# A later assumed landing for the block-diagonal loads in a hand-made instruction order

## The chip, the cores and the metric

The kernel runs on one core of one Trainium2 chip. The metric is the device time of one execution in microseconds (us); less is better.

## What is computed

Three stages follow one another. A delta-rule recurrence over 768 tokens (4 batches, 8 heads, head size 48), then two feed-forward layers over the 3072 token rows (384 to 2048 to 384), the first with a softplus, the second with h·cos(h) between its two products.

```python
def _attn_ref(q, k, v, beta):
    k_n = k / (np.linalg.norm(k, axis=-1, keepdims=True) + 1e-06)
    state = np.zeros((B, H, D, D))
    for t in range(S):
        y[:, :, t] = np.einsum('bhd,bhde->bhe', q[:, :, t], state)
        v_old = np.einsum('bhde,bhd->bhe', state, kt)
        state = state + bt[:, :, :, None] * np.einsum('bhd,bhe->bhde', kt, vt - v_old)

def _moe_ref(x, w_in, w_out):       # first layer
    h = x @ w_in
    return (np.maximum(h, 0.0) + np.log1p(np.exp(-np.abs(h)))) @ w_out

def _moe2_ref(x, w_in, w_out):      # second layer
    h = x @ w_in
    return (h * np.cos(h)) @ w_out
```

## The kernel before, in words

**The work.** The recurrence is cut into 24 chunks of 32 tokens. Six groups of four chunks are prepared: `norms` (L473) loads the keys into `kt` and squares them on ScalarE, `prep` (L946) normalizes, splits into fp16 pairs and transposes, loads `bdA`, forms the chunk's Gram products in `gram` (L572) and stores what the recurrence will need to DRAM (`kqd`, `kpd`), and `solve` (L620) inverts a triangular system on VectorE and stores it to `tgd`. `step(n)` (L696) then runs one chunk: a product with the state by `bdK`, two products with `bdT` with one by `bdG` between them, the state's update and an output by `bd2`, another by `bdQ`, and a DMA transpose of the output into `xt`. Two chunks make one block of 256 tokens for the first feed-forward layer (`moe_in`, `moe_out`; 12 blocks), and pairs of those blocks make the 6 blocks of the second.

**The block-diagonal operands.** Each chunk's per-head operands stand in SBUF as block-diagonal tiles, one 32-row block for each batch, so that one 128x128 matmul serves four batches. The zeros are written once. `bd_load` (L563) fills the four blocks with four DMAs from the SP queue; `load_G` (L665) does the same for `bdG` with lines of its own. There is one buffer of each tile, so a load waits until the last matmul on the old contents is done.

**The order.** Nothing is run where it is written. `put` collects every operation with its engine, an assumed duration and the keys that it writes and reads. `Plan.run` (L246) then makes one fixed order for each engine. `tails` (L119) gives each operation a priority: the assumed time from its start to the end of the program. `greedy` (L130) walks forward through assumed time and gives each engine, whenever it is free, the ready operation of highest priority. The walk is done six times, each with priorities from a walk backward over the last order, and the order with the shortest assumed span is emitted. The chip then runs each engine's list in order, with semaphores for the dependences.

For a DMA the plan assumes an issue of 0.475 to 0.65 us on SP, and data that stands 0.65 us, the transfer and 0.9 us after it, plus `slack`. In the forward walk `end = dma_free + 0.9 + o["slack"]` (L223) is when the readers may start; in `tails` and in the walk backward `0.65 + 0.9 + o["dma"] + o["slack"]` (L117) is added to the load's own priority, and so to that of all that comes before it. The transfers assumed are 0.45 us for `bdK` and `bdQ`, 0.35 for `bdA`, 0.22 for `bdT`, 0.67 for `bd2` and 0.11 for `bdG`. `slack` is 0 except for the transposes into `xt` (8 us from chunk 3 on).

Of the kernel before, what the change touches and what calls it, by code (L numbers as in the profile page):

```python
# [20 lines left out]
P = 128  # L21
B, H, S, D = 4, 8, 768, 48
C = 32
# [259 lines left out]
def delta_moe_moe_kernel(ctx, tc, q, k, v, beta, mask, w1, w2, out):  # L283
# [39 lines left out]
    bdG = att.tile([P, H, B, X2], F16, name="bdG")  # L323
# [6 lines left out]
    y16 = att.tile([P, 2, H, D], F16, name="y16")  # L330
# [36 lines left out]
    kpd = dr.tile([NS, P, C * 56], F16, name="kpd")  # L367
# [4 lines left out]
    def put(var, w, r, fn, **kw):  # L372
        return pl.add(var, w, r, fn, **kw)

    def dma(dst, src, w, r, eng_us, issue=0.475, **kw):
        put([("SP", issue)], w, r, lambda e: nc.sync.dma_start(out=dst, in_=src), dma=eng_us, **kw)  # L376

    def copy(out, in_, scale, w, r, n, ps=False, fast=True, only=None, **kw):
        var = [("ACT", act(n, ps)), ("DVE", dve(n, fast and not ps))]
        if only:  # L380
            var = [x for x in var if x[0] in only]

        def fn(e):
            if e == "ACT":
                nc.scalar.activation(out=out, in_=in_, func=AF.Copy, scale=scale)  # L385
            elif scale == 1.0:
                nc.vector.tensor_copy(out=out, in_=in_)
            else:
                nc.vector.tensor_scalar_mul(out, in_, scale)

        put(var, w, r, fn, port=fast, **kw)
# [7 lines left out]
    def stt(out, a, s, b, op0, op1, w, r, n, **kw):  # L399
        put([("DVE", dve(n) + (0.0 if isinstance(s, (int, float)) else 0.06))], w, r,  # L400
            lambda e: nc.vector.scalar_tensor_tensor(out, in0=a, scalar=s, in1=b, op0=op0, op1=op1), port=True, **kw)  # L401
# [13 lines left out]
    A = dict(boost=BOOST)  # L415
# [130 lines left out]
    def kqd_key(n, i):  # L546
        return [("kqd", n)] if n >= 4 else [("kqd", n, i)]
# [15 lines left out]
    def bd_load(dst, key, src, r, us, issue=0.475):  # L563
        src = src.rearrange("p (x t) -> p x t", t=X2)
        for b in range(B):
            rows = slice(32 * b, 32 * b + 32)
            dma(dst[rows, :, b], src[rows], [(key, b)], r + [(key, "z")], us, issue=issue, **A)

    def bk(key):
        return [(key, b) for b in range(B)]  # L570
# [91 lines left out]
    def load_T(n):  # L662
        bd_load(bdT, "bdT", tgd[n // 4, :, n % 4], [("tgd", n // 4)], 0.22)

    def load_G(n):  # L665
        src = kpd[n, :, 48 * C:].rearrange("p (h x) -> p h x", h=H)
        for b in range(B):
            rows = slice(32 * b, 32 * b + N2)
            dma(bdG[rows, :, b, C:], src[rows], [("bdG", b)], [("kpd", n), ("bdG", "z")], 0.11, **A)


    def load_v(n):
        dma(vtb[n % 2], v[n].rearrange("p (h d) -> p h d", h=H), [("vt", n % 2)], [], 0.55, **A)

    def group(ps, key, passes, first=True, last=True):
        for i, (lhs, mov, r) in enumerate(passes):
            def fn(e, i=i, lhs=lhs, mov=mov):
                for h in range(H):
                    nc.tensor.matmul(  # L679
                        ps[:, h, 0:D], lhsT=lhs(h), rhs=mov[:, h],  # L680
                        start=(first and i == 0 and h == 0),
                        stop=(last and i == len(passes) - 1 and h == H - 1))
            put([("PE", 8 * mm(D))], [key], r, fn, cold=1.55, **A)
# [4 lines left out]
    def by_state(bd, key):  # L688

        r = bk(key)  # L690
        return ([(lambda h, l=l: col(bd, H + h, l), st16[:, m, 0], r + [("st16", m, 0)])
                 for l, m in HI_FIRST]
                + [(lambda h, l=l: col(bd, h, l), st16[:, 1, 1], r + [("st16", 1, 1)])
                   for l in range(2)])

    def step(n):  # L696
        vk = [("vt", n % 2)]
        vt = vtb[n % 2]
        if n == 0:
            copy(bt, vt, -1.0, [("bt",)], vk, DM, **A)  # L700
        else:
            r = ps_c[0]
            group(r, ("psC", 0), by_state(bdK, "bdK"))
            stt(bt, r[:, :, 0:D], 1.0 / (K_SC * S_SC), vt, ALU.mult, ALU.subtract, [("bt",)],
                [("psC", 0)] + vk, DM, **A)
        if n + 1 < NS:
            bd_load(bdK, "bdK", kqd[n + 1, :, 0:32 * C], kqd_key(n + 1, 0), 0.45)

        def take_b():
            copy(b16[:, 0], bt, S_SC, [("b16", 0)], [("bt",)], DM, **A)  # L710
            stt(b16[:, 1], bt, S_SC, b16[:, 0], ALU.mult, ALU.subtract, [("b16", 1)], [("bt",), ("b16", 0)], DM, **A)

        take_b()
        if n:
            group(ps_y, ("psY",), by_state(bdQ, "bdQ"), last=False)
        if n + 1 < NS:
            bd_load(bdQ, "bdQ", kqd[n + 1, :, 32 * C:], kqd_key(n + 1, 1), 0.45)
        if n + 2 < NS:
            load_v(n + 2)
        if n and n % 4 == 0:  # L720
            load_T(n)
        u = ps_c[1]
        uk = [("psC", 1)]
        tk = bk("bdT")

        def take_u():
            copy(u16[:, 0], u[:, :, 0:D], 1.0 / T_SC, [("u16", 0)], uk, DM, ps=True, **A)
            stt(u16[:, 1], u[:, :, 0:D], 1.0 / T_SC, u16[:, 0], ALU.mult, ALU.subtract, [("u16", 1)],
                uk + [("u16", 0)], DM, **A)

        by_T = [(lambda h, l=l: col(bdT, h, l), b16[:, m], tk + [("b16", m)]) for l, m in HI_FIRST]
        group(u, ("psC", 1), by_T)
        take_u()
        x = ps_c[0]
        group(x, ("psC", 0), [(lambda h, l=l: col(bdG, h, l), u16[:, m], bk("bdG") + [("u16", m)])
                              for l, m in HI_FIRST])
        if n + 1 < NS:
            load_G(n + 1)
        stt(bt, x[:, :, 0:D], 1.0 / (K_SC * S_SC), bt, ALU.mult, ALU.add, [("bt",)], [("psC", 0)], DM, **A)
        take_b()  # L740
        group(u, ("psC", 1), by_T)
        if (n + 1) % 4:
            load_T(n + 1)
        take_u()
        if n + 1 < NS:
            for c in range(2):
                d = ps_c[c]
                group(d, ("psC", c), [
                    (lambda h, c=c, l=l: col(bd2, (1 - c) * H + h, l), u16[:, m],
                     bk("bd2") + [("u16", m)]) for l, m in HI_FIRST])  # L750
            for c in range(2):
                stt(st[:, c], ps_c[c][:, :, 0:D], 1.0 / K_SC, st[:, c], ALU.mult, ALU.add, [("st", c)],
                    [("psC", c)], DM, **A)
                copy(st16[:, 0, c], st[:, c], 1.0, [("st16", 0, c)], [("st", c)], DM, **A)
                if c == 0:
                    tt(st16[:, 1, c], st[:, c], st16[:, 0, c], ALU.subtract, [("st16", 1, c)],
                       [("st", c), ("st16", 0, c)], DM, **A)
                else:
                    stt(st16[:, 1, c], st16[:, 0, c], mask_sb[:, C:C + 1], st[:, c], ALU.mult, ALU.add,
                        [("st16", 1, c)], [("st", c), ("st16", 0, c), ("mask",)], DM, **A)  # L760
        group(ps_y, ("psY",), [(lambda h, l=l: col(bd2, 2 * H + h, l), u16[:, m],
                                bk("bd2") + [("u16", m)]) for l, m in HI_FIRST], first=(n == 0))
        if n + 1 < NS:
            load_2(n + 1)
        sc = Y_SC / (Q_SC * S_SC)
        copy(y16[:, 0], ps_y[:, :, 0:D], sc, [("y16", 0)], [("psY",)], DM, ps=True, **A)
        stt(y16[:, 1], ps_y[:, :, 0:D], sc, y16[:, 0], ALU.mult, ALU.subtract, [("y16", 1)],
            [("psY",), ("y16", 0)], DM, **A)
        j, off = blk_of[n]
        x = xtb[j % XTB]  # L770
        put([("SP", 0.65)], [("xt", j % XTB, i) for i in range(off // P, off // P + 1)],
            [("y16", 0), ("y16", 1)],
            lambda e: nc.sync.dma_start_transpose(
                out=x[:, :, off:off + P], in_=y16.rearrange("p a h d -> p (a h d)")), dma=0.67, hold=0.55, slack=8.0 if n > 2 else 0.0, **A)


    blocks = [[n, n + 1] for n in range(0, NS, 2)]
# [147 lines left out]
    for n in range(4):  # L925
        prep_k(n)
        if n % 2:
            dst, keys = (bdKQ[:, :, 0:12], bdA22)[n // 2], [first[n - 1][1], first[n][1]]
            src = kg0[n // 2][:, :, 16 * C:].rearrange("p n (x t) -> p n x t", t=X2)
            for m in range(2):  # L930
                for b in range(B):
                    rows = slice(32 * b, 32 * b + 32)
# [6 lines left out]
    for n in range(4):  # L939
        prep_q(n)  # L940
        ps, pk = gram(n, first[n][0], first[n][1], (1,))
        take_P(n, ps[:, :, 0], pk)
    load_2(0)
    load_G(0)

    def prep(n):  # L946
# [14 lines left out]
    for g in range(NG):  # L961
# [8 lines left out]
        for n in range(4 * g, 4 * g + 4):  # L970
            step(n)
            j, off = blk_of[n]
# [55 lines left out]
```

## Time and profile before

| | us |
|---|---|
| median of 3 runs | 1060.73 |
| lowest, highest | 1059.9, 1066.73 |
| the profiled execution's own time | 1063.94 |
| its span, first to last instruction | 1062.1 |

The page of the profile gives the busy time of each engine, the share of 40 slices, the chain that ended last and the costliest groups; the trace behind it answers which wait ended last before an instruction. PE is TensorE's matmuls, PEld its weight loads, DVE is VectorE, ACT ScalarE, POOL GpSimd, SPq the queue that issues the DMAs. `bdA` and `bd2` are parts of one tile, and so are `bdK` and `bdQ`; the trace tells them by the source: `bdA<-kq` is the load of `bdA`, `bdA<-kpd` that of `bd2`, `bdKQ<-kqd` those of `bdK` and `bdQ`. PE's granted clock is given as a share of 2.4 GHz.

### The profile page before, as it was taken

The page shows a single profiled execution, that of the slowest core. Times are in us where ns is not written, and L with a number is a line of the kernel's source. Part 1 is how long each engine was busy: PE and PEld are TensorE (multiplying, and loading weights), DVE is VectorE, ACT ScalarE, POOL GpSimd, SP SyncE. Part 2 cuts the span into 40 slices and gives each one's busy share as a digit, 9 for nine tenths or more (in the row PEclk, how much of TensorE's full clock was granted, in tenths as well). Part 3 has the DMA queues.
Part 4 walks back from the last instruction along what each step waited for, and adds up shares of the span by engine and source line. Part 5 has one row for each costly group of instructions (what it writes and reads, how often), then busy time and mean ns, then how long its engine had stood idle before and what let it go on. Part 6 is the DMA issues. An engine that isn't in the chain of part 4 may idle for free.

```text
span 1062.1 us, 27812 instructions
## 1 busy us (share of the span) xinstructions
PE 946.3 (89%) x11552; PEld 687.3 (65%) x11552; DVE 656.2 (62%) x1146; ACT 681.4 (64%) x1281; POOL 404.0 (38%) x365
## 2 busy tenths in 40 slices
PE   1246769898889899999999999999999999999998
PEld 1146648797778789889988998844444444444443
DVE  7876877566836683674485675497555555555554
ACT  5455748686757676777666877976555545555554
POOL 7363526433423352252223433555223323223332
PEclk9556978999989999999999999999999999999999
DMA  8888794758754876567477972111101000010000
GB/s 246 217 219 173 162 246 113 178 129 181 174 127 69 178 170 121 84 156 168 68 148 178 215 169 83 60 45 60 60 1 60 1 30 30 1 60 1 30 1 31
DMA packets 307742, 117.94 MB, mean 111 GB/s; under 512 B 272160, under 2 KB 287648, under 8 KB 307616
## 3 DMA queue, kind: packets, MB, share of 16 engines
q1 hardware_dynamic: 307616, 116.17, 46.2%
q8 instruction: 91, 1.49, 0.6%
q14 instruction: 35, 0.29, 0.1%
HBM read 71.03 MB, written 35.65 MB: 100 GB/s over the span
## 4 chain that ended last, share of the span: by engine, by line
PE 63%; DVE 9%; DMA 8%; SPq 7%; ACT 6%; issue 4%; POOL 2%; DVEq 0%; POOLq 0%; ACTq 0%
PE psH L798 18%; PE accA L860 12%; PE accB L860 9%; PE psC L798 7%; SPq L376 7%; PE psA L860 6%; PE psC L679 5%; PE psY L798 3%; PE psY L679 2%; DMA kt<-k_dram 2%; DMA bdA<-kq 1%; DMA kpd<-kp 1%; PE psA L589 1%; DVE tmpd L397 1%; DVE tlan L397 1%
## 5 line engine op out<-in xcount | busy, mean ns | idle before, releaser
L397 POOL TENSOR_TENSOR g<-g,g 128x512 f16<-128x512 f32 x192 | 227.4, 1185 | 499.1 <-ACT g L385 489.1
L798 PE MATMUL psH<-xt,w 128*128 128x256 f16 x1728 | 238.2, 278 | 7.6 <-DVE g L397 5.9
L385 ACT ACTIVATE g<-g 128x512 f16<-128x512 f32 x192 | 120.5, 629 | 104.4 <-DVE g L401 65.4
L798 PEld LDWEIGHTS <-w 128*128 128x128 f16 x1728 | 159.5, 99 | 28.3 <-issue 8.1
L860 PEld LDWEIGHTS <-w 128*128 128x128 f16 x1728 | 162.8, 98 | 21.2 <-issue 1.6
L860 PE MATMUL accA<-g,w 128*128 128x256 f16 x1152 | 159.0, 275 | 1.1 <-POOL g L397 1.0
L860 PEld LDWEIGHTS <-v 128*128 128x128 f16 x864 | 84.5, 98 | 102.1 <-issue 0.3
L798 PEld LDWEIGHTS <-v 128*128 128x128 f16 x864 | 84.5, 98 | 101.4 <-issue 0.8
L406 ACT ACTIVATE e<-e 128x512 f32<-128x512 f32 x96 | 60.3, 629 | 84.0 <-DVE e L401 84.0
L397 DVE TENSOR_TENSOR g<-psH,e 128x512 f32<-128x512 f32 x96 | 66.1, 688 | 67.1 <-ACT e L408 59.6
L860 PE MATMUL accB<-g,w 128*128 128x256 f16 x576 | 95.0, 275 | 0.0
L798 PE MATMUL psH<-xu,v 128*128 128x512 f16 x351 | 83.3, 379 | 0.6 <-DVE g L401 0.6
L798 PE MATMUL psC<-xu,v 128*128 128x512 f16 x342 | 81.5, 379 | 0.0
L679 PE MATMUL psC<-b,bdT 128*128 128x48 f16 x1152 | 44.1, 186 | 38.3 <-ACT bdT L385 18.9
L860 PE MATMUL accA<-g,v 128*128 128x512 f16 x288 | 78.0, 379 | 0.0
L860 PE MATMUL accB<-g,v 128*128 128x512 f16 x288 | 77.8, 379 | 0.0
L860 PE MATMUL psA<-g,v 128*128 128x512 f16 x288 | 77.6, 379 | 0.0
L679 PEld LDWEIGHTS <-bdKQ 128*128 128x128 f16 x1840 | 64.9, 99 | 15.1 <-issue 12.8
L815 ACT ACTIVATE e<-psH 128x512 f32<-128x512 f32 x96 | 56.8, 591 | 24.5 <-PE psH L798 23.6
L408 ACT ACTIVATE e<-e,hpi 128x512 f32<-128x512 f32 x96 | 69.1, 721 | 2.9
L679 PEld LDWEIGHTS <-bdT 128*128 128x128 f16 x1152 | 41.6, 99 | 42.2 <-issue 38.0
L679 PEld LDWEIGHTS <-bdA 128*128 128x128 f16 x1680 | 55.1, 99 | 9.1 <-issue 7.2
(128 smaller groups left out, 1550.0 us busy)
## 6 DMA issues: line engine op xcount, KB each, us to landing
bdKQ<-kqd SPq DMA_DIRECT2D x184, 64.0 KB, 2.9
kpd<-kp SPq DMA_DIRECT2D x24, 448.0 KB, 3.9
kqd<-kq SPq DMA_DIRECT2D x20, 512.0 KB, 4.5
raw<-w_dram SPq DMA_DIRECT2D x12, 768.0 KB, 6.0
bdA<-kpd SPq DMA_DIRECT2D x96, 96.0 KB, 3.7
w<-w_dram SPq DMA_DIRECT2D x10, 768.0 KB, 6.3
v<-w_dram SPq DMA_DIRECT2D x10, 768.0 KB, 4.8
qt<-q_dram SPq DMA_DIRECT2D x24, 256.0 KB, 3.7
```

Source lines behind the costliest of these rows:

```text
L376: put([("SP", issue)], w, r, lambda e: nc.sync.dma_start(out=dst, in_=src), dma=eng_us, **kw)
L385: nc.scalar.activation(out=out, in_=in_, func=AF.Copy, scale=scale)
L397: put(var, w, r, lambda e: eng[e].tensor_tensor(out=out, in0=a, in1=b, op=op), port=True, **kw)
L406: nc.scalar.activation(out=out, in_=in_, func=func, scale=scale)
L408: nc.scalar.activation(out=out, in_=in_, func=func, scale=scale, bias=bias)
L589: nc.tensor.matmul(ps[:, h], lhsT=w, rhs=x, start=(i == 0), stop=(i == len(ops) - 1))
L679: nc.tensor.matmul(ps[:, h, 0:D], lhsT=lhs(h), rhs=mov[:, h], start=(first and i == 0 and h == 0), stop=(last and i == len(passes) - 1 and ...
L798: nc.tensor.matmul(hp[:, i] if ph == 0 else hp, lhsT=w[:, l, kc * P:(kc + 1) * P], rhs=xv[:, m * KC + kc], start=(kc == 0 and idx == 0), s ...
L815: nc.scalar.activation(out=ev, in_=hv, func=AF.Abs, scale=sc)
L860: nc.tensor.matmul(acc[c], lhsT=w[:, l, c * P:(c + 1) * P], rhs=rhs, start=(f == 0 and idx == 0 and (ph == 1 or c != 1)), stop=(f == NF - ...
```

## The change

Three lines. `bd_load` and `load_G` now pass `slack=2` for each of their DMAs; the slack of the transposes is written 8 in place of 8.0, the same value. No operation is added or taken away, and none changes its size, engine choice or dependences. Only the plan's numbers change, and with them the order in which the same instructions are emitted. Not touched are the loads of `kt`, `qt`, `vt` and the weights, nor the loads of the first four chunks' `bdK` and `bdA`, which are written out with `dma` and not `bd_load`.

```diff
@@ bd_load
-            dma(dst[rows, :, b], src[rows], [(key, b)], r + [(key, "z")], us, issue=issue, **A)
+            dma(dst[rows, :, b], src[rows], [(key, b)], r + [(key, "z")], us, issue=issue, slack=2, **A)
@@ load_G
-            dma(bdG[rows, :, b, C:], src[rows], [("bdG", b)], [("kpd", n), ("bdG", "z")], 0.11, **A)
+            dma(bdG[rows, :, b, C:], src[rows], [("bdG", b)], [("kpd", n), ("bdG", "z")], 0.11, slack=2, **A)
@@ step
-                out=x[:, :, off:off + P], in_=y16.rearrange("p a h d -> p (a h d)")), dma=0.67, hold=0.55, slack=8.0 if n > 2 else 0.0, **A)
+                out=x[:, :, off:off + P], in_=y16.rearrange("p a h d -> p (a h d)")), dma=0.67, hold=0.55, slack=8 if n > 2 else 0.0, **A)
```

## Rows read from the trace of the kernel before

**Rows 1.** The page, section 1: busy us (share) and instructions of PE
```profile
PE 946.3 (89%) x11552; PEld 687.3 (65%) x11552; DVE 656.2 (62%) x1146; ACT 681.4 (64%) x1281; POOL 404.0 (38%) x365
```

**Rows 2.** Busy time by stretch of the span; the first line names the columns
```profile
core 0: us, PE busy (x) PEld busy (x) DVE busy (x) ACT busy (x) POOL busy (x), PEclk, DMA share, GB/s
0.00:98.00 98.00, 33.04 (x848) 31.13 (x849) 76.59 (x147) 51.69 (x110) 54.81 (x52) 0.69 0.83 218
98.00:200.00 102.00, 77.25 (x1211) 66.68 (x1211) 73.24 (x132) 67.76 (x138) 47.04 (x41) 0.88 0.75 171
200.00:650.00 450.00, 428.07 (x7446) 389.25 (x7446) 278.45 (x542) 323.69 (x663) 160.08 (x157) 0.98 0.67 147
650.00:1062.00 412.00, 407.97 (x2049) 200.22 (x2047) 227.91 (x329) 238.30 (x373) 142.06 (x116) 1.00 0.09 31
```

**Rows 3.** Waits of PE, whole span: us in total, times, longest us
```profile
PE psA L589 <- DMA bdA<-kq: 12.7, 9, 3.5
PE psC L679 <- DMA bdT<-tgd: 2.6, 5, 0.8
```

**Rows 4.** DMA issues: count, KB each, median us from issue to landing
```profile
bdKQ<-kqd SPq DMA_DIRECT2D x184, 64.0 KB, 2.9
bdA<-kpd SPq DMA_DIRECT2D x96, 96.0 KB, 3.7
kt<-k_dram SPq DMA_DIRECT2D x24, 192.0 KB, 3.9
bdA<-kq SPq DMA_DIRECT2D x80, 48.0 KB, 2.4
bdT<-tgd SPq DMA_DIRECT2D x92, 32.0 KB, 2.5
bdG<-kpd SPq DMA_DIRECT2D x96, 8.0 KB, 3.2
```

**Rows 5.** The tile bdA: its DMAs from issue to landing
```profile
DMA to landing us min/median/max: 2.0/3.2/8.2
```

**Rows 6.** Timeline of PE: start us, us, line, operation [idle before <-releaser]
```profile
82.07 2.32 PE L589 MATMUL psA<-kq,bdA 128*128 128x64 f16 x40 [3.48 <-DMA bdA<-kq]
98.47 3.33 PE L798 MATMUL psH<-xt,w 128*128 128x256 f16 x15 [1.71 <-DMA xt<-y]
444.60 0.78 PE L589 MATMUL psA<-kq,bdA 128*128 128x64 f16 x20 [2.05 <-DMA bdA<-kq]
```

**Rows 7.** Timeline before the first block: loads on SPq and their readers
```profile
62.72 3.93 SPq L376 DMA_DIRECT2D bdT<-tgd  x4
69.46 3.43 SPq L376 DMA_DIRECT2D bdA<-kpd  x4
74.62 1.12 PE L679 MATMUL psC<-b,bdT 128*128 128x48 f16 x24 [3.26 <-ACT b L385]
85.98 0.80 PE L679 MATMUL psC<-u,bdA 128*128 128x48 f16 x16 [0.63 <-ACT u L385]
```

**Rows 8.** Stretches of 5 us, columns as in rows 2
```profile
135.00:140.00 5.00, 0.00 (x0) 0.00 (x0) 1.68 (x5) 0.03 (x1) 0.00 (x0) 0.50 1.01 372
440.00:445.00 5.00, 2.95 (x68) 2.54 (x66) 4.03 (x6) 3.35 (x7) 1.97 (x3) 1.00 0.53 81
```

**Rows 9.** Waits of ACT, whole span, columns as in rows 3
```profile
ACT sq L406 <- DMA kt<-k_dram: 18.3, 4, 7.5
```

**Rows 10.** Timeline of three late key loads and of who waits
```profile
132.78 0.61 SPq L376 DMA_DIRECT2D kt<-k_dram  x1
139.97 0.52 ACT L406 ACTIVATE sq<-kt 128x384 f32<-128x384 f32 x1 [7.48 <-DMA kt<-k_dram]
141.69 1.12 PE L679 MATMUL psC<-b,bdT 128*128 128x48 f16 x24 [7.03 <-ACT b L385]
...
200.20 0.57 PE L679 MATMUL psC<-b,bdT 128*128 128x48 f16 x16 [3.68 <-ACT b L385]
...
307.54 0.80 PE L679 MATMUL psY<-u,bdA 128*128 128x48 f16 x16 [3.14 <-ACT u L385]
```

## The prediction

> **What bounds the kernel now.** I read the page first, then the busy time by stretch, then what ended PE's waits, and last the timeline around the longest of them. The page shows PE busy for 946.3 of 1062.1 us [rows 1], so the time is PE's work plus PE's gaps. The stretches say where those gaps are [rows 2]. In the first 98 us PE is busy for 33.0 and waits for the preparation of the first chunks; until its first feed-forward matmul at 98.47 [rows 6] there is little else that it could do. From 98 to 200 it idles 102.0 − 77.3 = 24.7 us, from 200 to 650 another 450.0 − 428.1 = 21.9, and from 650 on 4.0. The last stretch holds only the second layer; its loads are not those of the change, and its PE is full at a clock of 1.00. So the change can act on the 98 us before the first block and on 24.7 + 21.9 = 46.6 us of gaps after it, and on the clock, which was granted at 0.88 and 0.98 of 2.4 GHz in the two middle stretches.
>
> **What of those gaps the loads of the change make.** The waits of PE name them [rows 3]: 12.7 us in 9 waits for `bdA`, 2.6 us in 5 for `bdT`, together 15.3 us. For `bdK`, `bdQ`, `bd2` and `bdG` no wait of PE ends with the DMA outside the opening's loads that the diff leaves alone. The other gaps end with ScalarE or VectorE.
>
> **The change, part by part.** No instruction is added, removed or resized; the 8 for 8.0 is the same number and costs nothing. All that changes is the assumed landing, and by it the order.
>
> *The landing.* Counted from the end of an issue, the plan now takes 0.65 + 0.35 + 0.9 = 1.90 us for `bdA`, 1.77 for `bdT`, 2.22 for `bd2`, 1.66 for `bdG` and 2.00 for `bdK` and `bdQ`. The medians measured from issue to landing are 2.4, 2.5, 3.7, 3.2 and 2.9 [rows 4]: later by 0.5 to 1.5 us, and somewhat less if the issue's own time is inside. With 2 us more the plan is at 3.90, 3.77, 4.22, 3.66 and 4.00: above each median, below the worst of 8.2 [rows 5]. So today's order puts readers where the data is mostly not there yet, and the new one where it mostly is.
>
> *The readers move back.* A Gram product now stands in PE's list at the plan's landing. At 444.60 the list had come to it 2.05 us early, and at 82.07 it was 3.48 us early [rows 6]. The matmuls behind it could not pass, since PE works its list in order. With 2 us more the plan puts other work of PE in front. Between 98 and 650 there is such work: the 12 blocks' matmuls, which keep PE at 428 of 450 us. So moving a reader back costs nothing there; without that cover (before 98 us) it could cost up to 2 us for each load in the chain to the first `xt`. I see two such loads whose readers run late in it, those of `bdT` and `bd2` for the second chunk. The first is issued until 62.72 + 3.93 = 66.65, lands some 2.5 us later at about 69.2 and is read at 74.62; the second is issued until 72.89, lands at about 76.6 and is read at 85.98 [rows 4, 7]. Both readers start when ScalarE is done, over 5 us behind the landing, more than the 2 us added. Bounds of this cost: 0 and 4 us. I take 0.
>
> *How much of 15.3 comes back.* A wait is covered as far as it is not longer than the added 2 us. Only the one of 3.48 is clearly longer, by 1.5, so at most 15.3 − 1.5 = 13.8 us come back; at the other end 0, if PE reaches the next wait (for ScalarE or VectorE) just as much sooner. The second happens to a part: of the gaps after 98 us, less than 15.3 of 46.6 end with these loads, and an instruction that runs sooner often meets an operand that does not come sooner. I take a little over half, 8 us.
>
> *The clock.* A gap costs more if the clock falls behind it. In 440 to 445 us PE idled 2.05 us for `bdA`, and the clock stayed at 1.00; in 135 to 140, where PE did nothing at all, it was at 0.50, that is 1.2 GHz [rows 8]. The waits of the change are of the first kind. I add 0. The other bound: from 200 to 650 us the clock's whole loss is 0.02 × 450 = 9 us [rows 2], and the share of these waits in the gaps, 15.3 of 46.6, would make 3 us of it.
>
> *The loads go earlier.* Each load's priority rises by 2 × 0.95 = 1.9 us, and so does that of all before it, twice where two such loads follow (`kt`, then `bdA`, then `bdT` behind the solve: 3.8). On SP this puts loads ahead of weights. But a `bd` load also waits for the last reader of its one buffer, so it can seldom go out much sooner, and where it is put early in SP's list, it holds the `kt`, `qt`, `vt` and weight loads and the transposes behind it. Bounds: no gain, and the loss worked out in the third rival. I take 0, since the same raise lifts `kt` by more than the loads it must pass.
>
> *The sum.* The profiled execution took 1063.9 us; less 8 is 1055.9. It lies 3.2 above the median of the runs, 1060.7. On the median's scale the forecast is 1053.
>
> A page of the Trainium skill bears on the constant: "DMA: Bandwidth & Descriptors", section "Latency and other measured facts", says that HBM access takes 0.2 us on average and 2 us at high load, and that lighter load makes the fixed cost smaller. The trace agrees that the landing is not one number: 2.0 to 8.2 us for one tile [rows 5]. By that rule 2 us would cover the loaded case, and the sum would be nearer to all 13.8 us, 1047; with light load it would be too late.
>
> **The rivals.**
>
> *It changes nothing.* The order is shuffled, waits for `bdA` become waits for `b`, `u` and `st` from ScalarE, and the end stays: 1060 ± 4. For it speaks that two thirds of the gaps have other causes, against it that the waits for `bdA` come back in nearly every group.
>
> *More falls away than these waits (faster).* The longest gaps after 98 us are not those of the `bd` loads. `kt` loads land late, ScalarE sits in front of the square for 18.3 us in 4 waits [rows 9], and PE behind it for 7.03, 3.68 and 3.14 us [rows 10]. A higher priority of all preparation may send `kt` out sooner. If the 13.8 us come back and the two longest of these with them, it is 1060.7 − 13.8 − 7.0 − 3.7 = 1036. Against it: the square on ScalarE rises in priority with its load and still follows the assumed landing, which is not changed for `kt`.
>
> *The key loads come later (slower).* At 132.78 `kt` was issued into full DMA engines (share 1.01, 372 GB/s [rows 8]) and ScalarE stood for 7.48 us, PE for 7.03 [rows 10]. If `bd` loads are put ahead on SP and hold the first `kt` of each of the five groups as long as this one, PE loses 5 × 7.0 = 35 us in place of 7.0 + 3.7 + 3.1 = 13.8: 21 us more, so 1060.7 + 21 = 1082, or 1074 with the 8 us of the forecast. It is slower by over 1% from two such gaps more if nothing else is won (2 × 7.0 = 14), from three if 8 us are (21 − 8 = 13). For it: a plan that errs by 5 us in one load stops every engine, and the diff leaves this error in. Against it: `kt` rises by 3.8 us and the `bd` loads by 1.9.
>
> **How the numbers follow.** A measurement of this kernel can tell about 1% from no change, that is 1050.1 and 1071.3. The forecast (1047 to 1060, likeliest 1053) has 0.34, no change (1056 to 1064) 0.22, more falls away (1030 to 1047) 0.24, later key loads (1067 to 1082) 0.20. The forecast's lower edge adds a little to faster, the second rival's and the third's inner edges take as much away: faster 0.25, same 0.55, slower 0.20. From 1035 to 1077 about half of each outer rival is inside, which leaves out 2 in 10.
>
> **What would show it.** Right: PE's waits for `bdA` and `bdT` fall from 15.3 us to below 5; PE's busy time from 200 to 650 us rises by the same; the first feed-forward matmul stays within 3 us of 98.5; the medians from issue to landing stay. Wrong: the first feed-forward matmul later by over 4 us (the opening's chain does depend on the order of these readers); waits of ScalarE for `kt` far from 18.3 us, either way (the second or the third rival); the same 15.3 us, now in waits for `b`, `u` or `st` (the first).

## The result and the profile after

| | before | changed |
|---|---|---|
| median, us | 1063.1 (4 runs) | 1051.6 (4 runs) |
| lowest, highest | 1059.9, 1066.73 | 1049.49, 1052.47 |
| span of the profiled execution | 1062.1 | 1050.7 |

The ratio is 0.9888 with a 95% interval of 0.9847 to 0.9929: 1.1% faster, at the edge of what one comparison tells from no change. The forecast was 1053. Times are medians, of 4 to 10 executions of each new kernel, and executions of one kernel lie up to about 1% apart.

The page of the changed kernel: PE's busy time, the clock by fortieth of the span, and two rows of the DMA issues with the median time from issue to landing:

```profile
PE 943.0 (90%) x11552; PEld 687.6 (65%) x11552; DVE 661.6 (63%) x1147; ACT 679.7 (65%) x1281; POOL 408.0 (39%) x364
...
PEclk9987879989999999999999999999999999999999
...
bdKQ<-kqd SPq DMA_DIRECT2D x184, 64.0 KB, 2.9
...
bdA<-kpd SPq DMA_DIRECT2D x96, 96.0 KB, 3.5
```

The same from the DMA view of the changed kernel, where the list is longer:

```profile
kt<-k_dram SPq DMA_DIRECT2D x24, 192.0 KB, 3.3
...
bdA<-kq SPq DMA_DIRECT2D x80, 48.0 KB, 2.2
...
bdT<-tgd SPq DMA_DIRECT2D x92, 32.0 KB, 2.9
bdG<-kpd SPq DMA_DIRECT2D x96, 8.0 KB, 3.2
```

The same DMAs move the same bytes and land as late as before (2.4, 2.5 and 3.2 us for `bdA`, `bdT` and `bdG` [rows 4]). The order is new, and with it one choice of engine, since the plan chooses that as well: one conversion of a second-layer weight (L467, at 640 us) went from GpSimd to VectorE, 365 and 1146 instructions before [rows 1], 364 and 1147 now. So the sentence ahead of the prediction that no operation's engine changes is wrong by this one.

All of PE's waits for a DMA in the changed kernel (the rows of `<-w` are the opening's loads, which the diff does not touch):

```profile
PE psA L589 <- DMA bdKQ<-w: 21.1, 1, 21.1
PE psH L798 <- DMA xt<-y: 2.8, 1, 2.8
PE psH L589 <- DMA bdA<-w: 1.8, 1, 1.8
PE accA L589 <- DMA bdA<-w: 1.5, 1, 1.5
PE psH L589 <- DMA bdKQ<-w: 1.1, 1, 1.1
PE psC L679 <- DMA bdKQ<-kqd: 0.9, 1, 0.9
```

The 12.7 us for `bdA` and 2.6 for `bdT` [rows 3] are gone; 0.9 us for a load of the change is left. That is what the change says it does. But the time that these waits held is not simply returned. The first feed-forward matmul of the changed kernel, by its timeline:

```profile
92.99 5.58 PE L798 MATMUL psH<-xt,w 128*128 128x256 f16 x27 [2.83 <-DMA xt<-y]
```

It starts 5.5 us earlier than the one at 98.47 [rows 6]. From there to the end, before and after, by the busy time of the engines (columns as in rows 2), first of the kernel before:

```profile
98.47:1062.15 963.68, 913.28 (x10704) 656.16 (x10703) 579.12 (x999) 629.39 (x1171) 349.06 (x313) 0.98 0.43 100
```

and of the changed kernel:

```profile
92.99:1050.68 957.69, 912.13 (x10728) 658.69 (x10728) 584.64 (x1001) 630.01 (x1174) 353.22 (x313) 0.98 0.43 102
```

So the 11.5 us of the two profiled spans are three terms: 98.47 − 92.99 = 5.5 us of the opening (all up to the first feed-forward matmul); PE's gaps behind it, 963.68 − 913.28 = 50.4 against 957.69 − 912.13 = 45.6, that is 4.8; and 913.28 − 912.13 = 1.2 us of shorter busy time. In the same stretch PE's waits for ScalarE's `b` have grown. PE's waits in it, the kernel before:

```profile
PE psC L679 <- ACT b L385: 10.9, 3, 7.0
PE psA L589 <- DMA bdA<-kq: 8.2, 7, 2.0
PE psH L798 <- DVE g L397: 5.9, 4, 2.8
...
PE psC L679 <- DMA bdT<-tgd: 2.6, 5, 0.8
```

The largest in the changed kernel:

```profile
PE psC L679 <- ACT b L385: 19.9, 5, 7.3
PE psY L679 <- ACT u L385: 7.2, 4, 4.0
PE psC L679 <- DVE st L401: 4.8, 2, 3.6
```

In this stretch the kernel before had 10.8 us of waits for the loads of the change (`bdA` 8.2, `bdT` 2.6). All of them went, and the gap fell by 4.8: the rest stands as longer waits for other engines, `b` from 10.9 to 19.9 us above all.

### The profile page after: what moved, and what is told of

Read it like the earlier page. It is cut to its first block, busy times and chain, and to the rows that moved or that the text cites. A ratio compares the mean times of both kernels' runs of the same rounds, so it can differ in the third digit from the quotient of the medians.

```text
span 1050.7 us, 27821 instructions
## 1 busy us (share of the span) xinstructions
PE 943.0 (90%) x11552; PEld 687.6 (65%) x11552; DVE 661.6 (63%) x1147; ACT 679.7 (65%) x1281; POOL 408.0 (39%) x364
## 4 chain that ended last, share of the span: by engine, by line
PE 71%; DMA 4%; DVE 4%; ACT 4%; SPq 3%; issue 2%; POOL 1%; ACTq 0%; DVEq 0%; POOLq 0%
PE psH L798 20%; PE accA L860 15%; PE accB L860 10%; PE psC L798 7%; PE psA L860 6%; PE psC L679 6%; PE psY L798 4%; SPq L376 3%; PE psY L679 2%; DMA kpd<-kp 2%; DMA kt<-k_dram 1%; PE psA L589 1%; DMA qt<-q_dram 1%; DMA xt<-y 1%; ACT kp L385 1%
## 5 line engine op out<-in xcount | busy, mean ns | idle before, releaser
L798 PE MATMUL psH<-xt,w 128*128 128x256 f16 x1728 | 234.7, 278 | 8.2 <-DVE g L397 4.7
L860 PEld LDWEIGHTS <-v 128*128 128x128 f16 x864 | 84.6, 98 | 101.9
L798 PEld LDWEIGHTS <-v 128*128 128x128 f16 x864 | 84.5, 98 | 100.9
L679 PE MATMUL psC<-b,bdT 128*128 128x48 f16 x1152 | 43.7, 187 | 46.9 <-ACT b L385 27.5
L679 PEld LDWEIGHTS <-bdKQ 128*128 128x128 f16 x1840 | 64.7, 98 | 14.0 <-issue 11.5
L679 PEld LDWEIGHTS <-bdA 128*128 128x128 f16 x1680 | 57.3, 100 | 12.3 <-issue 10.3
```

The source lines that it names most:

```text
L679: nc.tensor.matmul(ps[:, h, 0:D], lhsT=lhs(h), rhs=mov[:, h], start=(first and i == 0 and h == 0), stop=(last and i == len(passes) - 1 and ...
L798: nc.tensor.matmul(hp[:, i] if ph == 0 else hp, lhsT=w[:, l, kc * P:(kc + 1) * P], rhs=xv[:, m * KC + kc], start=(kc == 0 and idx == 0), s ...
L860: nc.tensor.matmul(acc[c], lhsT=w[:, l, c * P:(c + 1) * P], rhs=rhs, start=(f == 0 and idx == 0 and (ph == 1 or c != 1)), stop=(f == NF - ...
```

## The experiments

Three theories were set against each other. **Landing**: PE's list comes to a reader before its data, and taking these waits away is the gain. **Priority**: the loads and the work before them go out earlier. **Reshuffle**: every engine's fixed order is new, and any new order lands within some 10 us of the old. "Gap" below is PE's idle time from its first feed-forward matmul to the end, "bd waits" the part of it that ended with a load of the change, and "all bd waits" the same over the whole span, the opening included; each is from the one profiled execution of the kernel. The ratio is to runs of the kernel before on the same chip, whose median there was 1063.1 to 1064.3 us; an interval without 1 in it shows a difference, and none of these differences reaches 2%.

| run | ratio, 95% | median us | first ff matmul | gap | bd waits in it | all bd waits |
|---|---|---|---|---|---|---|
| before | | 1063.1 | 98.5 | 50.4 | 10.8 | 15.3 |
| changed | 0.985–0.993 | 1051.6 | 93.0 | 45.6 | 0 | 0.9 |
| e1 readers | 1.001–1.007 | 1067.9 | 100.9 | 49.1 | 5.1 | 10.3 |
| e2 priority | 1.005–1.010 | 1072.6 | 100.8 | 53.2 | 1.0 | 30.7 |
| e3 bdA only | 0.997–1.001 | 1062.4 | 100.8 | 50.3 | 2.5 | 8.1 |
| e4 slack on v | 0.993–0.997 | 1059.7 | 93.5 | 49.6 | 10.8 | 12.7 |
| e5 Gram later, PE alone | 1.007–1.014 | 1072.2 | 97.3 | 53.1 | 12.2 | 17.5 |
| e6 changed opening | 0.997–1.002 | 1062.5 | 94.8 | 54.0 | 10.2 | 15.1 |
| e7 changed rest | 0.993–0.998 | 1056.6 | 98.4 | 46.7 | 4.6 | 9.3 |
| e8 kt too | 0.988–0.994 | 1051.7 | 96.7 | 41.6 | 1.9 | 1.9 |
| e9 base nudged | 0.995–1.001 | 1062.6 | 100.2 | 52.4 | 12.1 | 14.6 |
| e10 change nudged | 0.995–1.001 | 1062.2 | 104.7 | 37.9 | 3.6 | 9.5 |
| e11 slack 1 | 0.981–0.990 | 1049.5 | 96.0 | 37.4 | 2.6 | 5.3 |
| e12 slack 4 | 0.989–0.994 | 1056.5 | 101.9 | 40.0 | 0 | 1.9 |

### Half of the change: readers alone, priorities alone

e1, on the changed kernel:

```diff
-        return 0.65 + 0.9 + o["dma"] + o["slack"] if o["var"][0][0] == "SP" else 0.0
+        return 0.65 + 0.9 + o["dma"] + (0 if o["slack"] == 2 else o["slack"]) if o["var"][0][0] == "SP" else 0.0
```

> The 2 us count only in the walk forward (when readers may start), not in the priorities. Landing theory (the gain is that PE's list no longer comes to a reader before its data): PE's waits for bdA and bdT below 2 us as in the changed kernel, against 15.3 before, and 1048 to 1056 us. Priority theory (the gain is that loads and all preparation before them are ordered earlier): the waits may go, but the time stays at 1058 to 1066 and the first feed-forward matmul at 98 us. Reshuffle theory (any new order lands anywhere within some 10 us): no link between these waits and the time.

e2, on the changed kernel:

```diff
-                end = dma_free + 0.9 + o["slack"]
+                end = dma_free + 0.9 + (0 if o["slack"] == 2 else o["slack"])
```

> The 2 us count only in the priorities, not in when readers may start. Landing theory: PE's waits for bdA and bdT stay at 10 us or more and the time at 1057 to 1067. Priority theory: the waits stay or fall a little, the first feed-forward matmul starts near 93 us as in the changed kernel, and the time is 1048 to 1056. Reshuffle theory: anywhere from 1045 to 1075, without a link to the waits.

Neither half gains; both are slower, by 0.4 and 0.8%. In e1 the waits behind the opening fall by half, over the whole span by a third (15.3 to 10.3 us), and the time rises. In e2, with readers at the old landing and the Gram's priority raised, PE's list comes to a Gram product of the opening far ahead of its load. The timeline of e2:

```profile
61.02 1.23 PE L589 MATMUL psA<-kq,bdA 128*128 128x64 f16 x20 [26.45 <-DMA bdA<-kq]
```

PE stands there for 26.45 us. Not all of that is a loss: PE's next matmul in e2 needs ScalarE's `bdT`, which is late as well, and in the kernel before PE stood at this place for `bdT` alone. First before, then e2:

```profile
53.39 1.12 PE L679 MATMUL psC<-b,bdT 128*128 128x48 f16 x24 [18.86 <-ACT bdT L385]
```

```profile
62.64 1.12 PE L679 MATMUL psC<-b,bdT 128*128 128x48 f16 x24 [0.40 <-ACT bdT L385]
```

After the opening e2 has hardly a wait for these loads, and still one of the largest gaps: ScalarE's `b` alone makes 21.8 us of it. The waits of PE in e2 behind the first feed-forward matmul:

```profile
PE psC L679 <- ACT b L385: 21.8, 9, 10.9
PE psY L679 <- ACT u L385: 6.9, 3, 4.0
PE psC L679 <- ACT u L385: 4.1, 2, 3.6
```

So the priority theory is wrong as it stood. The landing theory is not refuted by e2, whose waits over the whole span doubled to 30.7 us; e1, 0.4% slower with a third of its waits gone, speaks against it. What was tried as one number has two sides, and neither did the work alone: the priority takes the load to be far from the end, and the walk then lets its reader wait. That the two must agree is my reading, with one order timed for each half.

### One load of six

```diff
-            dma(dst[rows, :, b], src[rows], [(key, b)], r + [(key, "z")], us, issue=issue, slack=2, **A)
+            dma(dst[rows, :, b], src[rows], [(key, b)], r + [(key, "z")], us, issue=issue, slack=2 if key == "bdA" else 0.0, **A)
-            dma(bdG[rows, :, b, C:], src[rows], [("bdG", b)], [("kpd", n), ("bdG", "z")], 0.11, slack=2, **A)
+            dma(bdG[rows, :, b, C:], src[rows], [("bdG", b)], [("kpd", n), ("bdG", "z")], 0.11, **A)
```

> The 2 us count for bdA alone, not for bdT, bdK, bdQ, bd2 and bdG. Landing theory: 12.7 of the 15.3 us of waits were for bdA, so most of the gain is here: bdA's waits near 0, bdT's 2 to 4, 1050 to 1057 us. Priority theory: only the preparation's priority rises, by 1.9 us; part of the gain, 1053 to 1060. Reshuffle theory: no rule, 1045 to 1075.

No wait for `bdA` is left, 12.7 us before, and the time is the same (0.9992). But a new wait for a load of the change stands in the opening, at 99.79 us, in front of the first feed-forward matmul, so that 8.1 of the 15.3 us remain. From e3's whole span:

```profile
PE psY L679 <- DMA bdKQ<-kqd: 5.6, 1, 5.6
```

The gap behind the opening is that of before to a tenth, 50.3 and 50.4. Its largest waits in e3:

```profile
PE psH L798 <- DVE g L397: 14.2, 5, 5.5
PE psC L679 <- ACT b L385: 13.0, 6, 5.1
PE psY L679 <- ACT u L385: 6.9, 2, 6.2
```

VectorE's `g`, 5.9 us before in the same stretch, is 14.2. The waits went to other operands. That is what the reshuffle theory said, and it is the miss that weighs most against my sum: 8.3 us of waits went from this stretch, and its gap stayed.

### The reader moved on PE and nowhere else

The order of before stays on DVE, ACT, POOL and SP; in PE's list the Gram products of the chunks from 4 on stand 2 us of planned time later.

```diff
+        log = self.plan(False)
...
+        late = {i for i, o in enumerate(self.ops) if o["var"][0][0] == "PE"
+                and any(self.ops[d]["bd"] and self.ops[d]["key"] in ("bdA",) for d in o["deps"])}
+        lists = {}
+        for st, end, e, i in log:
+            lists.setdefault(e, []).append((st + (2.0 if i in late else 0.0), len(lists.get(e, ())), i, e))
+        lists["PE"].sort()
...
```

> The order of before on DVE, ACT, POOL and SP to the last instruction; in PE's list alone the Gram products of the chunks from 4 on stand 2 us of planned time later, behind feed-forward work. Landing theory: PE's waits for bdA fall from 12.7 to 2 us or less, nothing else moves, and the time falls by 6 to 12 us, 1051 to 1058. Reshuffle theory (these waits are not what the end hangs on; the gap comes back at ScalarE's and VectorE's next results): the waits fall, and the time stays within 4 us of before, 1059 to 1067.

It missed both expectations: 1.0% slower, and the waits are still 12.2 us. The reason that the waits stayed stands in SP's list. `bdA` has one buffer, so the next load of it waits for the Gram product, and SP works its list in order. What SP waited for in the kernel before, whole span:

```profile
SPq L376 <- PE psA L589: 0.9, 3, 0.4
```

and in e5 (from 98 to 650 us, which holds all of it; the lines are numbered higher by 46):

```profile
SPq L422 <- PE psA L635: 8.4, 6, 2.4
```

With the Gram later, SP stood 8.4 us in place of 0.9 in front of the next `bdA` load, and the loads behind it came later too: PE's waits for `bdT` in the stretch went from 2.6 to 3.8 and one of 2.9 us for `bdG` was new. PE's waits in e5 behind its first feed-forward matmul:

```profile
PE psA L635 <- DMA bdA<-kq: 5.5, 5, 1.4
...
PE psC L725 <- DMA bdT<-tgd: 3.8, 3, 1.7
...
PE psY L725 <- DMA bdG<-kpd: 2.9, 1, 2.9
```

A reader that is moved moves the writer of its buffer's next contents, so this edit did not take the waits away and does not test what their removal gives. Nor do gaps make more than a part of the 1.0%: e5's profiled span is 6.6 us longer than before, by 2.7 us of gaps and 5.0 of longer PE busy time behind an opening 1.2 us shorter, and why the busy time rose is open.

### A sham, and a nudge

e4 puts the 2 us on the loads of `v` in place of the block-diagonal ones:

```diff
-            dma(dst[rows, :, b], src[rows], [(key, b)], r + [(key, "z")], us, issue=issue, slack=2, **A)
+            dma(dst[rows, :, b], src[rows], [(key, b)], r + [(key, "z")], us, issue=issue, **A)
-            dma(bdG[rows, :, b, C:], src[rows], [("bdG", b)], [("kpd", n), ("bdG", "z")], 0.11, slack=2, **A)
+            dma(bdG[rows, :, b, C:], src[rows], [("bdG", b)], [("kpd", n), ("bdG", "z")], 0.11, **A)
-        dma(vtb[n % 2], v[n].rearrange("p (h d) -> p h d", h=H), [("vt", n % 2)], [], 0.55, **A)
+        dma(vtb[n % 2], v[n].rearrange("p (h d) -> p h d", h=H), [("vt", n % 2)], [], 0.55, slack=2, **A)
```

> The order of before with the 2 us put on the loads of v alone, for which PE does not wait directly and whose landing nothing on PE waits for. Landing theory and priority theory: PE's waits for bdA and bdT stay at 10 us or more and the time within 5 us of before, 1057 to 1068. Reshuffle theory: the time moves by up to 10 us either way although no reader of a block-diagonal load is moved by its own slack.

It is 0.5% faster with its `bd` waits all there: 10.8 us behind the opening, as before. The gain lies in the opening, where its first feed-forward matmul came at 93.5, near the 93.0 of the changed kernel.

e9 and e10 take one number of the plan from 0.95 to 0.951, once without the change and once with it:

```diff
-BOOST = 0.95
+BOOST = 0.951
```

> The kernel before with one number of the plan nudged that means nothing on the chip: the weight on the recurrence's priorities 0.951 in place of 0.95. Every engine's order changes. Reshuffle theory: the time moves by 4 to 12 us, either way, and PE's waits for the block-diagonal loads move without it. Landing theory: these waits stay at 10 us or more (the plan still takes them to land too early), 1058 to 1068 us.

> The changed kernel with the same nudge, to be set against the nudged base. Landing theory: PE's waits for the block-diagonal loads are below 3 us again and the time is 7 to 14 us under the nudged base. Reshuffle theory: the waits are below 3 us, and the time lies anywhere within some 10 us of the nudged base, above it as well as below.

This pair decides how far the result may be carried. The nudge alone did nothing clear of noise (e9 against before, 0.995 to 1.001), where the reshuffle theory had 4 to 12 us. On the nudged base the same change gains nothing: 1062.6 and 1062.2 us. But its two parts are large and opposed. The stretch behind the first feed-forward matmul, of e9:

```profile
100.15:1066.36 966.21, 913.79 (x10760) 657.82 (x10759) 586.81 (x1008) 631.84 (x1176) 348.96 (x314) 0.98 0.43 100
```

and of e10:

```profile
104.69:1058.87 954.18, 916.29 (x10700) 659.42 (x10699) 583.12 (x996) 627.91 (x1170) 350.43 (x311) 0.98 0.42 100
```

The gap falls from 52.4 to 37.9 us, by three times as much as in the change itself, while the opening grows by 4.5 us and the busy time by 2.5. By these single profiles the span still falls by 7.5 us; by the ten runs of each the two kernels are equal. The profiled execution of e9 was the longest of its ten, 5.5 us above their median, that of e10 lay 1.6 below, and the split by parts is that uncertain. Both theories had the waits of e10 below 3 us. They are not: over the whole span 9.5 us remain of e9's 14.6, most of them in the opening, where PE waited for `bdA` with the 2 us in the plan. From e10's whole span:

```profile
PE psA L589 <- DMA bdA<-kq: 5.9, 2, 4.6
...
PE psY L679 <- DMA bdG<-kpd: 3.6, 1, 3.6
```

### The opening and the rest, joined from two orders

e6 takes the changed kernel's order up to the first planned feed-forward matmul and the order of before for what is left; e7 the other way round.

```diff
+    def joined(self, a, b):
+        head = a[:self.opening(a)]
+        done = {x[3] for x in head}
+        return head + [x for x in b if x[3] not in done]
```

> The changed kernel's order up to its first planned feed-forward matmul, then the order of before for all that is left. Opening theory (half of the gain is that the changed order brings the first feed-forward matmul from 98.5 to 93.0 us, and PE is full enough afterwards to keep it): first matmul at 92 to 95 us and 1054 to 1060 us in all. If the opening's lead is lost in later waits: first matmul as early, but 1061 to 1067.

> The order of before up to its first planned feed-forward matmul, then the changed kernel's order. Opening theory: first matmul at 97 to 101 us, the later 6 us of the gain stay, 1055 to 1061. If the whole gain is one of the order after 98 us: 1049 to 1055. If neither half keeps its gain without the other: 1061 or more.

e6 starts its feed-forward work at 94.8 us, and the lead is lost: 1062.5, gap 54.0. e7 starts at 98.4 as before did, and keeps 0.45 of the 1.1%: 1056.6, gap 46.7. So a part of the gain lives in the order behind the opening, as the gaps say (in e7's profile 3.7 us of gap, and 4.7 of shorter PE busy time as well). That the rest needs both parts from one plan is a reading, not shown: a joined order is a third order.

### The size, and the other late load

e11, and e12 with 4 in place of 1:

```diff
-            dma(dst[rows, :, b], src[rows], [(key, b)], r + [(key, "z")], us, issue=issue, slack=2, **A)
+            dma(dst[rows, :, b], src[rows], [(key, b)], r + [(key, "z")], us, issue=issue, slack=1, **A)
-            dma(bdG[rows, :, b, C:], src[rows], [("bdG", b)], [("kpd", n), ("bdG", "z")], 0.11, slack=2, **A)
+            dma(bdG[rows, :, b, C:], src[rows], [("bdG", b)], [("kpd", n), ("bdG", "z")], 0.11, slack=1, **A)
```

> 1 us in place of 2 in both places. Landing theory: the planned landings (2.7 to 3.2 us) come near the measured medians of 2.2 to 3.7; PE's waits for these loads 2 to 6 us, 1051 to 1058. Reshuffle theory: waits as low, the time anywhere from 1048 to 1070.

> 4 us in place of 2. Landing theory: no waits for these loads below what 2 us left (0.9 us), so no further gain; the chain before the first feed-forward matmul may lengthen by up to 2 us for each of its loads; 1051 to 1058. Reshuffle theory: waits near 0, the time anywhere from 1048 to 1070.

Both are faster than before, by 1.5 and 0.9%, with gaps of 37.4 and 40.0. e11 has the lowest median of all, 1049.5, but its interval, 0.981 to 0.990, overlaps that of the change.

e8 adds the loads of `kt`:

```diff
-            dma(kt, k[n].rearrange("p (h d) -> p h d", h=H), kk, [("pre",)], 0.55, **A)
+            dma(kt, k[n].rearrange("p (h d) -> p h d", h=H), kk, [("pre",)], 0.55, slack=2, **A)
```

> The changed kernel with the same 2 us counted for the loads of kt too, whose late landing holds ScalarE for 11.7 us and PE behind it in the changed kernel. Landing theory carried on: ScalarE's waits for kt fall below 5 us, and 1042 to 1049 us. Reshuffle theory: ScalarE's waits for kt fall, the time lands anywhere within 10 us of the changed kernel, 1042 to 1062.

1051.7 us: no gain over the change. ScalarE's waits for `kt` did not fall below 5 us, as the landing theory had it. The change, then e8:

```profile
ACT sq L406 <- DMA kt<-k_dram: 11.7, 7, 5.1
```

```profile
ACT sq L406 <- DMA kt<-k_dram: 10.9, 3, 6.7
```

### What the runs say together

Behind the opening one rule holds over all orders that were timed. With the 2 us (or 1, or 4) on all six loads and in both places the gap is 37.4 to 45.6 us in five kernels; in the three with none on them (before, e4, e9) it is 49.6 to 52.4; in the three with a part of the change 49.1 to 53.2; in e5 to e7 it goes with the order of the later part, 53.1 and 54.0 with that of before, 46.7 with the changed one. Were the whole distance of each profiled execution from its kernel's median put down to the gap, the five would be at 38.5 to 44.7 us and the three at 46.9 to 49.6, still apart. Two things weaken the rule. A late opening may leave less to wait for behind it: the start of the first feed-forward matmul and the gap, added, are 133.4 to 142.6 us in the five and 143.1 to 152.6 in the three, apart by 0.5. And PE's busy time in this stretch, for nearly the same matmuls, went from 908.6 us (e7) to 918.3 (e5), a spread of 9.7 us beside 16.6 of the gaps; nothing here explains it.

In this stretch the `bd` waits fall in the full and in the partial orders alike, which made them look like no measure of the time. Over the whole span they are a better one. The four kernels with 0.9 to 5.3 us of them (changed, e8, e11, e12) are the four fastest, at 0.985 to 0.991 of before; the ten with 8.1 to 30.7 us all lie at 0.995 or above (the nearest two, e12 and e4, overlap in their intervals). The parts, the joined orders and e10 had waits for these loads in the opening. So the landing theory fits the set better than the single runs made it look: e4 and e9, with the 2 us on none of these loads, kept their waits and stayed within 0.5% of before, as it said. It is not shown. The waits were not varied alone (e5 tried to and did not), e1 and e3 lost waits and gained nothing, not all waits of the opening are a loss (e2), and each row is one profile.

The length of the opening does not follow the change at all: the first feed-forward matmul came at 98.5, 93.5 and 100.2 us without it and at 93.0, 96.7, 104.7, 96.0 and 101.9 with it. I take its 5.5 us of the measured 11.5 for chance of the order, which is argued and not shown: e7, with the opening of before, kept less than half of the gain, which agrees; e6, with the changed opening, gained nothing, which does not. It is the order's, at least, and not that of one execution: e7 and e6 repeat the two openings, at 98.4 and 94.8 us.

## Why the prediction was right, point by point

**The number was right and its bookkeeping half.** The forecast was a gain of 8 us from 1060.7, the measured gain is 11.5 from 1063.1; that 1051.6 comes so near to 1053 is luck in part, since a fourth run had moved the median of before by 2.4 us. 8 us were to come back from PE's gaps. PE's idle time over the whole span fell from 1062.15 − 946.32 = 115.8 to 1050.68 − 943.02 = 107.7, by 8.1. But 3.3 of it lie in the opening, and only 4.8 where I had placed the gain. The sign that I had named for it, PE's busy time from 200 to 650 us up by as much as the waits fell, did not come: 428.07 [rows 2] became 430.25, by 2.2. The changed kernel:

```profile
200.00:650.00 450.00, 430.25 (x7391) 392.57 (x7390) 284.09 (x547) 324.54 (x664) 167.86 (x159) 0.98 0.65 147
```

**The landing.** Right for this order. The medians stayed within 0.4 us, and with the planned landing above them PE's waits for these loads are 0.9 us, below the 5 that I had named. In e10, with the same 2 us, 9.5 were left.

**Readers move back at no cost, since PE has other work.** Wrong as a rule. e5 showed what I had left out: the next load waits for that reader, and SP behind that load.

**A little over half comes back.** The step that was nearest, by its reason as well: 4.8 of the 10.8 us of waits behind the opening, the rest turned into waits for `b` and `st`. But in this stretch e3 and e2 took nearly as much away (8.3 and 9.8) and got nothing, and e10 got 14.5 from 8.5. A share of the waits was a guess at the size, not a mechanism.

**The opening.** I took 0 with a cost of at most 4 us; it gave 5.5, and in e10 it cost 4.5. This is the term that was mis-sized: it needed a range of both signs. I had read the two loads whose readers come late, and they did not matter; what moved was the order of the rest. I named a start within 3 us of 98.5 as a sign of being right and a shift by more than 4 us later as one of being wrong; it shifted earlier, by 5.5.

**The clock.** I added 0 and bounded it at 3 us. Busy time fell by 3.3, of which 913.28 − 912.13 = 1.2 behind the opening and the rest in it, where 24 matmuls fewer ran (11552 − 10728 = 824 in place of 848). In the changed kernel up to 93 us:

```profile
0.00:50.00 50.00, 9.18 (x320) 8.87 (x320) 38.03 (x84) 23.95 (x54) 28.03 (x31) 1.00 0.81 236
50.00:93.00 43.00, 21.72 (x505) 20.01 (x506) 38.91 (x63) 25.71 (x54) 26.75 (x21) 0.82 0.81 199
```

The clock was granted at 1.00 and 0.82, where the first 98 us of before had 0.69 on average [rows 2], with as little PE work. It cannot be put down to the change: the last section shows the clock to differ between executions of one kernel.

**The rivals.** "It changes nothing" is what e3 did, with the mechanism that I gave it: waits for `bdA` became waits for ScalarE and VectorE. e10 kept the time of its base too, but otherwise: its gap fell, and its opening and its busy time rose. In the changed kernel itself that mechanism took 6.0 of the 10.8 us behind the opening. "More falls away" was half there: ScalarE's waits for `kt` fell from 18.3 us [rows 9] to 11.7 without a change to `kt`, which I had listed as a sign of being wrong. "The key loads come later" was not seen; the median of `kt` went from 3.9 to 3.3 us. The page "DMA: Bandwidth & Descriptors" of the Trainium skill ("Latency and other measured facts": HBM access slower at high load) had led to nearly all 13.8 us, 1047: the cover was as full as that rule would have it in this order, and the time did not follow all the way.

## What to carry to other kernels

Where one program fixes the order of five engines, the price of a wait in the trace does not say what its removal gives: e3 got nothing from 8.3 us, e10 14.5 us of gap from 8.5. A new order takes waits away and puts others in, so count them over the whole span, also where the change was not expected to act. Judge such a change on more than one base (a nudge of a number that means nothing is a cheap second base), by the stretch that it should act on and by the whole time. And where a reader is planned later, look at who waits for that reader, the next load of its buffer and the queue behind it.

## What was not expected of the hardware

The granted clock of the opening differs between the profiles, at nearly the same PE work: 0.80 and 0.57 in the two halves of the 98.5 us of before, 1.00 and 0.82 after. The two halves of before:

```profile
0.00:50.00 50.00, 9.09 (x320) 8.75 (x320) 39.59 (x86) 23.48 (x53) 29.72 (x31) 0.80 0.84 230
50.00:98.47 48.47, 23.95 (x529) 22.38 (x530) 37.47 (x63) 28.57 (x57) 25.22 (x22) 0.57 0.82 204
```

PE was busy for 9.09 and 9.18 us in the first 50 us of the two kernels, at 0.80 and at 1.00 of 2.4 GHz. The order alone does not make it: e6, which takes the changed kernel's order for the opening, had 0.79 there, and 0.62 from 50 to 94 us. The mean clock of whole executions differs within one kernel too, 0.959 to 0.976 in the four of the changed one. In 20 executions of the kernel before on one chip it was 0.952 to 0.965 ten times and 0.971 to 0.981 ten times, and the time did not go with it: the medians are 1064.3 and 1064.1 us. No run here tells what sets it.
